# Attention and MLP on one core: batch 0 with products of zeros on TensorE, its masks and first bias rows made by TensorE, and loads issued head by head

## Chip, cores, metric

One Trainium2 chip, one NeuronCore. Times are device microseconds of a whole execution. The profiler's span of the same execution is shorter (390.0 beside 391.85). On one core, runs have no slow and fast die to compare; all runs here are of the state "fast", and yet those of one kernel spread by up to 6 us (before: 390.3 to 396.2).

## The reference, cut to what matters

```
# q, k, v: (8, 8, 576, 64), s: (8, 8, 576)
scores = q @ k.T / sqrt(D)
cum  = cumsum(max(s, 0)); bias = -(cum[i] - cum[j])        # "rows" c below
scores = where(causal, -1e9, scores + min(bias, 0))
attn = softmax(scores) @ v
x  = attn, heads side by side                               # (8, 576, 512)
xn = (x - mean) / sqrt(var + 1e-6) * g_ln
out = x + max(xn @ w_ch1, 0) @ w_ch2                        # 512 -> 2048 -> 512
```

## The kernel before

A head n (0 to 63) is: `scores` (products sa, sb, sc and sd of the four key blocks, exponentials by ScalarE), then, two heads later, `pv` (the weighted sum, into one PSUM buffer `pot`). From head 10 on, four MLP units of the batch before are woven into each head, so batch 0 (heads 0 to 7) and heads 8 and 9 stand alone. `qk_pair` transposes q and k of the next two heads. The bias enters as extra rows of q and k: cumulative sums split into c_hi, c_mid, c_lo.

```
def aug(gam, eng, last=None):            # bias rows of four heads: 4 DMAs, here from GpSimd
    eng.dma_start(out=kq[i][D+1:D+2, 0, :, 0:S], in_=c_hi[r0:r0+G, :])   # ... three more
def qk_pair(g, k_eng, q_eng):
    tr = ps_t.tile([P, S], BF16, name="trqk", tag="tr")      # ps_t: 2 buffers, also sd and trx
    ...                                                      # 6 transposes, 2 copies by eng
def scores_d(b, j):
    ...                                                      # 2 products, 1 exponential
    nc.gpsimd.affine_select(out=ed, in_=ed, ...)             # mask on GpSimd
...
aug(0, nc.gpsimd, nc.scalar)                                 # c_lo's row from ScalarE's queue
for n in range(BH):
    pre(n)                                                   # loads, casts, fills of that head
    if n < 10:
        scores(b, h)
        if h % 2 == 0: scores_d(b, h // 2)
        if n % 2 == 0 and n < 8:
            g = n // 2 + 1
            qk_pair(g, "dve", "dve" if g % 2 else "act")
        if n == 9:
            for t in range(NF): ln_tr(0, t)                  # transposes of xn
            queue += batch_units(0)                          # MLP units of batch 0
        if n > 1: pv_next()
        if n == 8: pv_next(); qk_pair(5, "act", "act")
        continue
    ...                                                      # cut: heads 10 to 63
```

The softmax here doesn't subtract the row's maximum and nothing guards it: scores larger than these inputs give would overflow.

## Time and profile before

| | before |
|---|---|
| median of the first runs | 393.6 us |
| span of the profile | 390.0 us |
| first score (sa of head 0) | 13.07 us |
| scores of head 8 | 39.65 us |
| first product of the MLP | 50.97 us |
| TensorE busy, share of the span | 92% |

Read the last line with care: busy is not fast. The clock column gives TensorE's granted clock, but here it reads 1.00 until its first recorded change at 39.53 us; before that the speed has to be read from distances between starts (from sa to its mask 0.40 us for head 5, 0.22 for head 8), as the prediction does. The lines are in the prediction.

### The profile page before, as it was taken

What the parts mean: (1) busy time and instruction counts of PE and PEld (TensorE: products, weight loads), DVE (VectorE), ACT (ScalarE), POOL (GpSimd) and SP (SyncE); (2) the same over time, 40 slices, a digit from 0 to 9 for tenths busy, and PEclk for the clock granted to TensorE, in tenths of its full rate; (3) what the DMA queues carried; (4) which work ended last, traced back from release to release, by engine and by line L of the source; (5) the groups of instructions that cost most, each with busy time, mean ns of one, the idle gap of its engine ahead of it and who ended that gap; (6) DMA issues with size and microseconds to landing.
All of it is one profiled execution on the core that took longest, in us unless ns stands there. A gap on an engine that the chain in (4) does not pass through costs nothing.

```text
span 390.0 us, 8129 instructions
## 1 busy us (share of the span) xinstructions
PE 360.7 (92%) x2959; PEld 199.4 (51%) x2959; DVE 202.5 (52%) x530; ACT 189.7 (49%) x359; POOL 177.6 (46%) x473
## 2 busy tenths in 40 slices
PE   1598699897999999999999999999999979999994
PEld 0376555454555555555555555655555534444441
DVE  7347745859643745484437545843665483212211
ACT  3476758574685356436743774277337400411400
POOL 5897359465656264636466656454742110000000
PEclk9999879999999999999999999999999989999998
DMA  8999799256886898749896998599820011002013
GB/s 190 223 155 206 132 129 152 30 105 155 184 180 125 143 242 184 173 118 234 180 166 158 236 177 195 141 213 170 195 92 4 2 54 55 2 28 81 2 34 73
DMA packets 148335, 51.84 MB, mean 133 GB/s; under 512 B 134696, under 2 KB 143496, under 8 KB 148296
## 3 DMA queue, kind: packets, MB, share of 16 engines
q1 hardware_dynamic: 139168, 44.07, 51.9%
q0 software_dynamic: 9120, 7.25, 12.5%
q8 instruction: 23, 0.38, 0.4%
q14 instruction: 16, 0.13, 0.1%
q10 hardware_dynamic: 8, 0.00, 0.0%
HBM read 37.11 MB, written 9.44 MB: 119 GB/s over the span
## 4 chain that ended last, share of the span: by engine, by line
PE 79%; DVE 10%; DMA 5%; ACT 2%; SPq 1%; issue 1%; POOL 0%; ACTq 0%; DVEq 0%
PE py L448 30%; PE ph L430 27%; PE pot L343 7%; PE sa L274 3%; PE sb L274 3%; PE sc L274 3%; DVE xn L401 2%; DVE kq L96 2%; PE trx L417 2%; DMA vtmp<-in_v_dram 2%; PE trqk L227 1%; SPq L149 1%; DMA kq<-c_lo 1%; DMA kq<-rows 1%; ACT er L285 1%
## 5 line engine op out<-in xcount | busy, mean ns | idle before, releaser
L448 PE MATMUL py<-w_bf,hT 128*128 128x512 bf16 x576 | 137.9, 381 | 2.5 <-DVE yo L457 2.2
L430 PE MATMUL ph<-xT,w_bf 128*128 128x512 bf16 x512 | 122.7, 381 | 1.2 <-DVE hT L438 1.0
L440 ACT ACTIVATE hT<-ph 128x512 bf16<-128x512 f32 x107 | 64.0, 598 | 83.4 <-PE ph L430 82.7
L430 PEld LDWEIGHTS <-w_bf 128*128 128x128 bf16 x576 | 52.1, 98 | 55.2 <-issue 5.6
L448 PEld LDWEIGHTS <-hT 128*128 128x128 bf16 x576 | 52.1, 98 | 52.5 <-issue 3.6
L285 ACT ACTIVATE er<-sa 128x512 bf16<-128x512 f32 x64 | 38.1, 596 | 79.2 <-PE sa L274 48.1
L293 POOL TENSOR_SCALAR_AFFINE_SELECT er<-er 128x128 bf16<-128x128 bf16 x216 | 59.5, 300 | 31.2 <-ACT er L285 31.0
L438 DVE TENSOR_SCALAR hT<-ph 128x512 bf16<-128x512 f32 x37 | 25.6, 691 | 58.0 <-PE ph L430 55.2
L161 POOL CAST rows<-rowtmp 128x512 bf16<-128x512 f32 (+1 forms) x50 | 30.5, 610 | 48.9 <-DMA rowtmp<-in_q_dram 46.2
L274 PEld LDWEIGHTS <-kq 68*128 68x128 bf16 x440 | 34.7, 102 | 34.6 <-POOL v_bf L98 5.5
L343 PEld LDWEIGHTS <-er 128*128 128x128 bf16 x960 | 40.0, 102 | 15.2 <-DVE xm L360 2.1
L351 DVE RECIPROCAL rinv<-pot 128x5 f32<-128x5 f32 x64 | 12.4, 194 | 61.1 <-PE pot L343 60.9
L343 PE MATMUL pot<-v_bf,er 128*128 128x65 bf16 x960 | 42.4, 199 | 1.7 <-DVE xm L360 1.7
L285 ACT ACTIVATE er<-sc 128x512 bf16<-128x512 f32 x64 | 38.9, 608 | 0.3
L285 ACT ACTIVATE er<-sb 128x512 bf16<-128x512 f32 x64 | 38.2, 596 | 0.0
L457 DVE SCALAR_TENSOR_TENSOR yo<-py,rstd,xb 128x512 f32<-128x512 f32 x32 | 23.8, 748 | 25.5 <-PE py L448 20.3
L98 POOL CAST v_bf<-vtmp 128x512 bf16<-128x512 f32 (+1 forms) x40 | 24.3, 616 | 17.4 <-DMA vtmp<-in_v_dram 17.3
L274 PE MATMUL sa<-kq 68*128 68x512 bf16 x64 | 26.5, 414 | 6.1 <-DMA kq<-c_lo 5.4
L353 DVE TENSOR_TENSOR xb<-pot,rinv 128x256 f32<-128x256 f32 x64 | 27.2, 425 | 2.2
L274 PE MATMUL sc<-kq 68*128 68x256 bf16 (+1 forms) x208 | 27.9, 244 | 0.1
L96 DVE COPY kq<-trqk 64x576 bf16<-64x576 bf16 x24 | 19.2, 800 | 14.9 <-PE trqk L227 14.5
L274 PE MATMUL sb<-kq 68*128 68x64 bf16 (+1 forms) x168 | 26.7, 261 | 0.2
(81 smaller groups left out, 301.9 us busy)
## 6 DMA issues: line engine op xcount, KB each, us to landing
vtmp<-in_v_dram SPq DMA_DIRECT2D x32, 256.0 KB, 4.2
out_dram<-yo SPq DMA_DIRECT2D x32, 256.0 KB, 2.2
rowtmp<-in_k_dram SPq DMA_DIRECT2D x40, 128.0 KB, 3.0
rowtmp<-in_q_dram SPq DMA_DIRECT2D x40, 128.0 KB, 3.2
w_bf<-in_moe_w_ch_dram POOLq DMA_DIRECT2D x8, 512.0 KB, 9.2
kp<-in_k_dram POOLq DMA_DIRECT2D x10, 144.0 KB, 4.1
qp<-in_q_dram POOLq DMA_DIRECT2D x10, 144.0 KB, 4.8
vtmp<-in_v_dram SPq DMA_DIRECT2D x8, 128.0 KB, 3.2
```

The source lines that it names most:

```text
L96: nc.vector.tensor_copy(out=out, in_=in_)
L98: nc.gpsimd.tensor_copy(out=out, in_=in_)
L161: nc.gpsimd.tensor_copy(out=r[0:pn, :, :, 0:D], in_=loaded.pop(("rows", gam, t))[0:pn])
L274: nc.tensor.matmul(a[:, c + a0 - q0 : c + a1 - q0], lhsT=k_cols(b, h, kb), rhs=cols, start=True, stop=not (pe_mask and diag),)
L285: nc.scalar.activation(out=e[:, o : o + 512], in_=a, func=ACT.Exp, scale=scale)
L293: nc.gpsimd.affine_select(out=e[:, o : o + P], in_=e[:, o : o + P], compare_op=ALU.is_ge, fill=0.0, base=0, pattern=[[1, P]], channel_mult ...
L343: nc.tensor.matmul(pot[:, t, :], lhsT=e[:, o : o + P], rhs=vv[:, kb, h, :], start=(kb == 0), stop=(kb == last),)
L353: nc.vector.tensor_tensor(out=xb[b][:, :, hs], in0=pot[:, 0:NF, 0:D], in1=rinv[:, 0:NF].unsqueeze(2).to_broadcast([P, NF, D]), op=ALU.mult,)
L430: nc.tensor.matmul(ph, lhsT=w1_bf[:, kd, fb * P : (fb + 1) * P], rhs=xT[:, kd, :], start=(kd == 0), stop=(kd == KD - 1),)
L438: nc.vector.tensor_scalar_max(out=hT[:, fb, :], in0=ph, scalar1=0.0)
L440: nc.scalar.activation(out=hT[:, fb, :], in_=ph, func=ACT.Relu)
L448: nc.tensor.matmul(py[0], lhsT=hT[:, fb, t * P : (t + 1) * P], rhs=w2_bf[:, fb, :], start=(fb == 0), stop=(fb == FB - 1),)
```

## The change

Intent: let TensorE's clock be granted early, by products of zeros while it would wait; make head 0's bias rows by small products instead of a DMA; take the masks of sd off GpSimd; and issue the loads in smaller portions. The diff, cut to its core:

```
+    def keep_warm(n):
+        w = ps_t.tile([P, 512], F32, name="idle", tag="tr")
+        for _ in range(n):
+            nc.tensor.matmul(w, lhsT=zeros[:, 0:P], rhs=zeros, start=True, stop=True)
@@ start
+    keep_warm(9)
-    aug(0, nc.gpsimd, nc.scalar)
+    aug(0, nc.sync, h0=1)                                   # heads 1 to 3 only
     qk_pair(0, "dve", "act")
+    # head 0: rows by 8 products with `pick`, keep_warm(4) among them, 4 copies out of PSUM
+    keep_warm(5)
@@ qk_pair:  batch 0 and pairs 4, 5 in the MLP's PSUM banks
+            if g < 6: tr = ps_m.tile([P, S], BF16, name="trqk", tag="m")
@@ scores_d: masks of batch 0 by a product with maskT, no affine_select
@@ pre(n):   aug on SyncE; one load per head (w1 at 0, 2, 4, 6; v of batch 1 at 6; w2 at 7 to 10)
+        elif n == 1:
+            nc.vector.memset(kq[1][D:KA, 1].bitcast(F32), ONE2)   # was GpSimd's, at n == 0
+            aug(1, nc.sync)
@@ loop
-                qk_pair(g, "dve", "dve" if g % 2 else "act")
+                qk_pair(g, "dve", "act")
+            if n < 8: keep_warm(2)
-            if n > 1: pv_next()
+            if n > 1 and n != 9: pv_next()                  # head 8's pv moves behind two units
             if n == 8: pv_next()
+                keep_warm(5)
```

More of the change, by code (lines that the diff above doesn't have):

```diff
@@ L87 @@
     xTm = const.tile([P, KD, 512], BF16, name="xTm")
-    c_hi = const.tile([BH, S], BF16, name="c_hi")
-    c_mid = const.tile([BH, S], BF16, name="c_mid")
-    c_lo = const.tile([BH, S], BF16, name="c_lo")
+    c3 = const.tile([BH, 3, S], BF16, name="c3")
+    c_hi, c_mid, c_lo = (c3[:, j, :] for j in range(3))
+    zeros = const.tile([P, 512], BF16, name="zeros")
+    ones = const.tile([BH, S], BF16, name="ones")
+    pick = const.tile([BH, 4, P], BF16, name="pick")
     def copy_on(eng, out, in_):
@@ L188, in ld_w2, with aug @@
         )
-    def aug(gam, eng, last=None):
-        r0 = gam * G
+    def aug(gam, eng, h0=0):
+        r = slice(gam * G + h0, gam * G + G)
         i = gam % 2
-        eng.dma_start(out=kq[i][D + 1 : D + 2, 0, :, 0:S], in_=c_hi[r0 : r0 + G, :])
-        eng.dma_start(out=kq[i][D : D + 1, 1, :, 0:S], in_=c_hi[r0 : r0 + G, :])
-        eng.dma_start(out=kq[i][D + 2 : D + 3, 0, :, 0:S], in_=c_mid[r0 : r0 + G, :])
-        (last or eng).dma_start(
-            out=kq[i][D + 3 : D + 4, 0, :, 0:S], in_=c_lo[r0 : r0 + G, :]
-        )
+        eng.dma_start(out=kq[i][D : D + 1, 1, h0:G, 0:S], in_=c_hi[r, :])
+        for j in range(3):
+            eng.dma_start(out=kq[i][D + 1 + j : D + 2 + j, 0, h0:G, 0:S], in_=c3[r, j, :])
     def bias_rows():
@@ L223, in qk_pair @@
             src = ready.pop((kind, g))
-            tr = ps_t.tile([P, S], BF16, name="trqk", tag="tr")
+            if g < 6:
+                tr = ps_m.tile([P, S], BF16, name="trqk", tag="m")
+            else:
+                tr = ps_t.tile([P, S], BF16, name="trqk", tag="tr")
             for t in range(QT):
@@ L304, in scores_d @@
         u0 = (2 * j) % 4
+        pe_mask = b * H + 2 * j < NM
         ed = er[0:TL, u0 : u0 + 2, OD : OD + TL]
@@ L312, in scores_d @@
                 start=True,
-                stop=True,
+                stop=not pe_mask,
             )
+            if pe_mask:
+                nc.tensor.matmul(
+                    d[:, u, :], lhsT=ident, rhs=maskT[:, 0:TL], start=False, stop=True
+                )
         nc.scalar.activation(out=ed, in_=d[0:TL], func=ACT.Exp, scale=scale)
+        if pe_mask:
+            return
         nc.gpsimd.affine_select(
@@ L504 @@
         ld_pair("q", g)
-    ld_v(0, 0)
-    ld_v(0, 1)
+    for t in range(3):
+        ld_v(0, t)
     ONE2 = 1.0019378662109375
     NEG2 = -1.0058441162109375
+    nc.vector.memset(zeros.bitcast(F32), 0.0)
     nc.vector.memset(warm, 0.0)
     nc.scalar.activation(out=warm[:, 1:2], in_=warm[:, 0:1], func=ACT.Exp)
+    keep_warm(9)
     nc.vector.memset(c_one, 1.0)
+    nc.vector.memset(pick.rearrange("p j m -> p (j m)").bitcast(F32), 0.0)
+    for j in range(3):
+        nc.vector.memset(pick[0:1, j, j + 1 : j + 2], 1.0)
+    nc.vector.memset(pick[0:1, 0, 32:33], 1.0)
+    nc.vector.memset(pick[0:1, 3, 0:1], -1.0)
+    nc.vector.memset(ones.bitcast(F32), ONE2)
     nc.vector.memset(kq[0][0:KA, 0, :, S:SP], 0.0)
-    nc.vector.memset(kq[0][D:KA, 1].bitcast(F32), ONE2)
+    nc.scalar.copy(
+        out=kq[0][D:KA, 1, :, 0:S], in_=ones[0:4].unsqueeze(1).to_broadcast([4, G, S])
+    )
     make_identity(nc, ident)
@@ L526 @@
     nc.gpsimd.memset(kq[0][D : D + 1, 0].bitcast(F32), NEG2)
+    ld_cast_pair(2)
     def v_edges(i):
@@ L544 @@
     nc.vector.tensor_tensor(out=c_lo, in0=c_in, in1=c_mid, op=ALU.subtract)
-    aug(0, nc.gpsimd, nc.scalar)
+    aug(0, nc.sync, h0=1)
+    ld_v(0, 3)
     qk_pair(0, "dve", "act")
-    ld_v(0, 2)
-    ld_v(0, 3)
+    ba = ps_s.tile([P, 512], F32, name="ba", tag="s")
+    bb = ps_s.tile([P, 512], F32, name="bb", tag="s")
+    for j, src in ((3, ones), (0, c_hi), (1, c_mid), (2, c_lo)):
+        if j == 2:
+            keep_warm(4)
+        nc.tensor.matmul(
+            ba, lhsT=pick[:, j, :], rhs=src[:, 0:512], start=(j == 3), stop=(j == 2)
+        )
+    for j, src in ((3, ones), (0, c_hi), (1, c_mid), (2, c_lo)):
+        nc.tensor.matmul(
+            bb[:, 0:TL], lhsT=pick[:, j, :], rhs=src[:, 512:S], start=(j == 3), stop=(j == 2)
+        )
+    nc.vector.tensor_copy(out=kq[0][D:KA, 0, 0, 0:512], in_=ba[0:4])
+    nc.scalar.copy(out=kq[0][D : D + 1, 1, 0, 0:512], in_=ba[32:33])
+    nc.vector.tensor_copy(out=kq[0][D:KA, 0, 0, 512:S], in_=bb[0:4, 0:TL])
+    nc.scalar.copy(out=kq[0][D : D + 1, 1, 0, 512:S], in_=bb[32:33, 0:TL])
+    keep_warm(5)
     cast_pair("k", 1, "pool")
@@ L551 @@
     ld_v(0, 4)
-    ld_cast_pair(2)
+    ld_cast_pair(3)
     v_edges(0)
@@ L555 @@
         cast_v(0, t, "pool")
-    nc.sync.dma_start(out=gb, in_=moe_g_ln.partition_broadcast(P))
     nc.gpsimd.memset(er[TL:P, :, OD : OD + TL], 0.0)
@@ L562, in pre @@
         if n == 0:
-            ld_cast_pair(3)
-            nc.gpsimd.memset(kq[1][D : D + 1, 0].bitcast(F32), NEG2)
-            nc.gpsimd.memset(kq[1][D:KA, 1].bitcast(F32), ONE2)
-            nc.gpsimd.memset(kq[1][0:KA, 0, :, S:SP], 0.0)
             nc.vector.memset(mhalf, -0.5)
+            nc.vector.memset(kq[1][0:KA, 0, :, S:SP], 0.0)
+            nc.vector.memset(kq[1][D : D + 1, 0].bitcast(F32), NEG2)
+            ld_w1(0)
         elif n == 1:
-            aug(1, nc.gpsimd)
+            nc.vector.memset(kq[1][D:KA, 1].bitcast(F32), ONE2)
+            aug(1, nc.sync)
             ld_cast_pair(4)
         elif n == 2:
-            ld_w1(0)
+            nc.sync.dma_start(out=gb, in_=moe_g_ln.partition_broadcast(P))
+            ld_w1(1)
+        elif n == 3:
             v_edges(1)
-            ld_v(1, 0), ld_v(1, 1), ld_v(1, 2), ld_v(1, 3), ld_v(1, 4)
-        elif n == 3:
-            ld_cast_pair(5)
-        elif n == 4:
+        elif n == 4:
+            ld_w1(2)
+        elif n == 5:
+            ld_cast_pair(5)
+        elif n == 6:
+            ld_w1(3)
+            ld_v(1, 0), ld_v(1, 1), ld_v(1, 2), ld_v(1, 3), ld_v(1, 4)
+        elif n == 7:
+            ld_w2(0)
+        elif n == 8:
+            ld_cast_pair(6)
+            ld_w2(1)
             cast_v(1, 0, "pool")
             cast_v(1, 1, "pool")
-        elif n == 5:
-            ld_w1(1)
+        elif n == 9:
+            ld_w2(2)
             cast_v(1, 2, "pool")
@@ L584, in pre @@
             cast_v(1, 4, "pool")
-        elif n == 6:
-            ld_cast_pair(6)
-        elif n == 7:
-            ld_w1(2)
-            ld_w1(3)
-        elif n == 9:
-            ld_cast_pair(7)
-            ld_w2(0)
-        elif n == 10:
-            ld_w2(1)
-            ld_w2(2)
-        elif n == 11:
+        elif n == 10:
+            ld_cast_pair(7)
             ld_w2(3)
@@ L609, in pre @@
         if n % 4 == 0 and 2 <= n // 4 + 1 < 2 * NPE:
-            aug(n // 4 + 1, nc.gpsimd)
+            aug(n // 4 + 1, nc.sync)
         for gam in range(2 * NPE, NG):
@@ L656 @@
                 g = n // 2 + 1
-                qk_pair(g, "dve", "dve" if g % 2 else "act")
+                qk_pair(g, "dve", "act")
+            if n < 8:
+                keep_warm(2)
             if n == 9:
@@ L661 @@
                 queue += batch_units(0)
-            if n > 1:
+            if n > 1 and n != 9:
                 pv_next()
@@ L675 @@
         run_units(1)
-        if n != 10:
-            pv_next()
+        pv_next()
         pend.append((b, h))
```

## The prediction

> **What bounds the kernel now.** I read the page's forty slices first, then the busy time by stretch, then the instructions in order of time up to 56 us, and last the chain that ended last.
>
> ```profile
> PE   1598699897999999999999999999999979999994
> PEclk9999879999999999999999999999999989999998
> DMA  8999799256886898749896998599820011002013
> ```
>
> One digit is 9.75 us. From the sixth slice on the PE row is nearly all nines: the MLP keeps TensorE full, and what lies there can't be shortened by this change. Room is in the first five slices, before the first product of the MLP (50.97 us). The stretches from 5.40 us, of 3.41 us each (start:end, length, PE busy, count, granted clock, DMA share, GB/s):
>
> ```profile
> 22.47:25.88 3.41, 3.40 (x37) 1.00 0.91 121
> 25.88:29.29 3.41, 3.10 (x32) 1.00 0.92 129
> ...
> 36.12:39.53 3.41, 3.41 (x42) 1.00 1.27 214
> 39.53:42.95 3.42, 2.49 (x53) 1.00 1.25 213
> 42.95:46.36 3.41, 1.79 (x25) 1.00 0.80 132
> 46.36:49.77 3.41, 2.30 (x28) 0.50 0.01 2
> 49.77:53.19 3.42, 3.42 (x15) 0.50 0.80 94
> ```
>
> Busy PE is not fast PE. The clock column says 1.00 up to 46 us, yet the timeline shows the products at half speed until 39.5 us (start us, duration):
>
> ```profile
> 29.68 0.62 PE L274 MATMUL sa<-kq 68*128 68x512 bf16 x1
> 30.08 0.31 PE L282 MATMUL sa<-maskT,ident 128*128 128x128 bf16 x1
> ...
> 39.65 0.38 PE L274 MATMUL sa<-kq 68*128 68x512 bf16 x1
> 39.87 0.22 PE L282 MATMUL sa<-maskT,ident 128*128 128x128 bf16 x1
> ```
>
> From sa to its mask takes 0.40 us for head 5 and 0.22 us for head 8: the clock column has no entry before its first change, and TensorE ran cold from the start to 39.5 us, again from 46.36 to 53.19. So batch 0 (heads 0 to 7, 13.07 to 39.65 us, 26.6 us, 6.65 a pair of heads) is bound by a cold TensorE, and the first score waits for something else:
>
> ```profile
> 13.07 0.59 PE L274 MATMUL sa<-kq 68*128 68x512 bf16 x1 [5.36 <-DMA kq<-c_lo]
> ...
> 44.94 2.66 DVE L401 SCALAR_TENSOR_TENSOR xn<-xb,mv,gb 128x512 bf16<-128x512 f32 x4
> 48.68 0.85 DVE L422 COPY xT<-trx 128x512 bf16<-128x512 bf16 x2 [0.34 <-PE trx L417]
> ```
>
> The bias rows come by DMA, 4.7 us after their issue at 8.15. Between head 8 and the MLP the bound is VectorE: weighted sums of heads 6 and 7, statistics, xn, xT, 40.75 to 49.5 us.
>
> [...] the changes at 39.53, 46.36 and 53.19 lie two windows of 3.413 us apart, release followed windows that were wholly busy (3.41, 3.42), one with 3.10 did not release, and 1.79 busy of 3.41 throttled while 1.94 (from 90.74) did not. [...] Up to 44 us the DMA share here is 0.9 to 1.3[...].
>
> **The change part by part.** All cold and warm costs are distances between starts in the timeline.
>
> *Start.* Nine products of zeros (9 x 0.427 = 3.8 us cold, from about 1.2 us when their zeros are written) end before the first transposes (5.9), and hold a whole window only for one phase in eight (3.84 - 3.41 of 3.41). Head 0's rows no longer come by DMA but by products: q's transposes end at 7.6 as now; then three products of 512 (1.28), four of zeros (1.71), the c_lo product (0.43), four of 64 columns (0.2), five of zeros (2.1): 13.3 us if cold, hardly better than 13.07. These 5.7 us are unbroken, so a free-running window fills somewhere between 10.5 and 13.9; after that the rest takes half. First score between 12.0 and 13.3, mean 12.6: gain 0.5 us. The copies out of PSUM (VectorE free at 9.7, c_lo product, 0.6 and 0.3) end by 12.0 and don't bind. The 2304-wide copy of ones on ScalarE (about 2.2 us, estimated from 0.60 for 512 and 0.83 for 768) ends near 5.1, about when k's load allows the cast anyway (5.02).
>
> *Heads 0 to 7, warm.* Per pair, TensorE: scores with masks 2 x 0.9, sd with its new masks 0.2, twelve transposes 0.52, two weighted sums 2 x 0.46, four products of zeros 4 x 0.215: 4.3 us. ScalarE: six exponentials at the 0.485 spacing of head 8 (40.19, 40.68, 41.16), sd 0.27, q's copies 1.61: 4.8. VectorE: k's copies 1.6, two heads of 0.98, statistics 0.9 to 1.4: 4.4 to 5.0. So the bound passes from TensorE (6.65) to ScalarE and VectorE at about 4.9, for all four pairs, as all q copies are now on ScalarE. Following the queues by hand from 12.8, with one weighted-sum buffer, scores(8) can start at 32.3 instead of 39.65. The masks of sd leave GpSimd (0.3 us each), which was no bound.
>
> *Taken back in there.* The bias rows of heads 4 to 7 wait on VectorE for a fill that now stands behind k's copies (about 17 us by my count), are then issued four times 0.52 us and land 3.4 to 6.9 us after (range in the trace): 22.5 to 25. Head 4 would want them at 22.0. I put down 1.2 us for that, and 0.3 for waits I can't see: scores(8) at 33.7.
>
> *Head 8 to the MLP.* The VectorE chain stays: 10.78 us from the exponentials of head 8 (40.19) to the MLP (50.97). Weighted sums of head 8 move behind the first two units: cold they took 0.84 us on the path, later they cost 0.46 warm. Five products of zeros fill only 1.1 us of a stretch where about 3.9 us of TensorE time hold 1.0 us of work; I expect the clock to be throttled there again in most phases, and 1.5 to 2.5 us lost on it, as now ((53.19 - 48.06) / 2 = 2.5). First MLP product about 10.3 us after scores(8): 44.0.
>
> *After.* TensorE is full from there, as many products as before plus the weighted sum moved: 50.97 - 44.0 - 0.46 = 6.5 us, rounded to 6.6 for a slightly shorter cold stretch: 393.6 - 6.6 = 387.0. The loads "one head at a time": only program order paces GpSimd's issues, and with the sd masks gone nothing holds it; four loads of weights enter the queue between about 16 and 22 us instead of 23.9 to 37.7.
>
> **Rivals.**
> (1) *DMA takes over.* Up to 45 us the engines are busy at a share near 1.2, with the same bytes needed 7 us earlier, and the last pair of q and k (issued behind three weight loads) is wanted near 36.6 us; my count has it landing between 31 and 36.5. For: GB/s falls to 121 only in one stretch, so there is little slack. Against: the weights of the later blocks (w2) aren't needed until 66 us, and v of batch 1 not until 45. If it binds, 2 to 5 us of the gain are lost: 389 to 391.
> (2) *The products of zeros cost more than they give.* If the window does not fill before head 0, cold pairs cost 6.4 + 4 x 0.43 = 8.1 us[...].
> (3) *The clock stays up throughout.* If the five products carry it over the xn stretch, some 2 us more are won, and with the bias rows in time another 1.2: 383 to 384. For it speaks that 1.94 us of work in a window sufficed.
> (4) *The gain is given back later.* In the region of 250 to 272 us the chain runs through row loads (vtmp, rows); but SyncE's queue there waits for outputs made by TensorE, so it moves with the start, and TensorE was busy 110 of 110 us from 140 to 250. I count little for it.
>
> **Range and chances.** The middle, 387.0, is the sum. Everything good (3) gives 383, DMA or bias rows late give 391. Two per cent is 385.8, within 1.2 us of my number: faster 0.35, same 0.63, slower 0.02, as only a fault that I don't see could cost over 14 us net.
>
> **What would show it.** Right: from sa to its mask 0.22 us from head 0 or 1 on; first score at 12 to 13.3; scores(8) at 32.5 to 35; exponentials of heads 2 to 7 back to back on ScalarE except ahead of head 4, where TensorE waits for the kq rows; first MLP product at 43 to 45; a granted clock of 0.50 at some time between 40 and 48; the MLP part unchanged in length. Wrong: a cold head 0 to 3, waits of trqk on kp or qp (rival 1), a first MLP product outside 42 to 46, or a gain at the end that differs from the gain at the first MLP product by over 1.5 us.

50.97 - 44.0 - 0.46 is 6.5 us, put at 6.6, and 393.6 - 6.6 = 387.0. Rival (2) came to 389. That another issuer of the bias rows shortens no transfer was not shown. The windows are the stretches of 3.413 us between which the clock changes in the traces (last section). That a filled one releases it was read from two of them (3.41 and 3.42 us of work), so what the *Start* says of it (one phase in eight, filled between 10.5 and 13.9, a first score as early as 12.0) is the author's estimate from these.

## The result

Median 387.44 us (387.33 to 387.59, 4 runs) beside 393.26 (391.32 to 393.66, 4 runs): ratio 0.9862, interval 0.9828 to 0.9896. A ratio here is the mean of one kernel's runs over the mean of the other's of the same rounds, so not quite the ratio of the medians. A second set of six runs gave 0.9869 (0.9823 to 0.9915; medians 387.56 and 392.61). By the 2% rule: the same; by the interval: faster by 1.0 to 1.7%.

The page after, the lines that answer to those of before:

```profile
PE   7878798997999999999999999999999979999994
PEclk9889899999999999999999999999999989999999
DMA  8799996178795599759887996589620011002013
```

The first, second and fifth slices of PE are fuller, the clock now has 8s in slices 2, 3 and 5 (the dips are in the record, as the first change comes early), and the rest is as before. From sa of head 0 to its mask:

```profile
12.14 0.38 PE L276 MATMUL sa<-kq 68*128 68x512 bf16 x1
12.36 0.22 PE L284 MATMUL sa<-maskT,ident 128*128 128x128 bf16 x1
...
24.46 0.38 PE L276 MATMUL sa<-kq 68*128 68x512 bf16 x1 [2.40 <-DMA kq<-c]
...
28.17 0.62 PE L276 MATMUL sa<-kq 68*128 68x512 bf16 x1
28.57 0.31 PE L284 MATMUL sa<-maskT,ident 128*128 128x128 bf16 x1
```

0.22 us: head 0 is warm. Head 4 (24.46) waits 2.40 us for its bias rows, and head 5 (28.17 to 28.57, 0.40) is cold again. The stretches of 3.41 us, laid so that their ends fall on the changes of the clock, show why (columns as in the prediction):

```profile
1.51:4.93 3.42, 3.42 (x9) 1.00 0.78 212
4.93:8.34 3.41, 2.06 (x18) 1.00 1.11 258
8.34:11.75 3.41, 3.41 (x13) 0.50 1.27 237
...
21.99:25.41 3.42, 1.02 (x14) 1.00 1.19 178
25.41:28.82 3.41, 3.41 (x39) 0.50 1.14 189
28.82:32.23 3.41, 3.41 (x53) 1.00 1.22 194
...
42.47:45.89 3.42, 1.74 (x18) 1.00 1.22 198
45.89:49.30 3.41, 3.41 (x21) 0.50 1.24 232
```

(Up to the first recorded change, here at 4.93 us, the column reads 1.00 while the products run at half speed, 0.43 us each, where four of 512 columns take 0.86 at full speed; the first of these stretches is the nine products of zeros.) A stretch with 1.02 or 1.74 us of work is followed by one at half clock; here a full one ends it. Busy time in the trace does not sort the stretches, though: one with 2.06 us (4.93 to 8.34) was also followed by half clock, one with 1.94 in the kernel before (from 90.74) was not, and there a stretch with 3.40 of 3.41 us of work (22.47 to 25.88) did not release the clock. More of them are at the end of this document; what sorts them is not shown.

Where the time went, in stretches between starts of sa, from each kernel's one profile. The last five columns are experiments that follow. Between heads 20 and 63 all are within 0.4 us of each other, so the whole matter is decided outside it. These are single profiles: those of f and c are of their slowest runs (388.76 us, 3.4 above the median of f, and 387.38), that of a is of its second slowest (388.82), that of j of its fastest.

| us | before | after | a no zeros | c rows early | f w2 late | j best | k gaps only |
|---|---|---|---|---|---|---|---|
| start to head 0 | 13.07 | 12.14 | 11.37 | 13.24 | 13.37 | 12.15 | 11.51 |
| head 0 to 8 | 26.58 | 23.40 | 24.80 | 19.64 | 19.38 | 19.73 | 22.65 |
| 8 to 11 | 16.44 | 16.67 | 17.53 | 17.60 | 17.35 | 14.50 | 14.37 |
| 11 to 14 | 15.16 | 15.15 | 15.16 | 15.15 | 15.15 | 13.96 | 13.97 |
| 14 to 18 | 16.52 | 16.52 | 16.52 | 18.19 | 16.52 | 16.53 | 16.52 |
| 18 to 20 | 12.07 | 12.08 | 12.07 | 12.08 | 15.13 | 12.10 | 12.08 |
| 20 to 63 | 204.07 | 203.82 | 203.84 | 203.83 | 204.19 | 203.79 | 203.82 |
| 63 to end | 86.09 | 85.92 | 85.81 | 85.87 | 85.91 | 84.24 | 84.18 |
| span | 390.0 | 385.7 | 387.1 | 385.6 | 387.0 | 377.0 | 379.1 |

Before to after: 0.93 us at the start and 3.18 in heads 0 to 8, and nothing between heads 8 and 14. By the profiles 4.3 us are won, and 5.8 by the medians.

### The profile page after: what moved, and what is told of

It reads as the page before. It is cut to its first block, busy times and chain, and to the rows that moved or that the text cites. A ratio compares the mean times of both kernels' runs of the same rounds, so it can differ in the third digit from the quotient of the medians.

```text
span 385.7 us, 8249 instructions
## 1 busy us (share of the span) xinstructions
PE 363.9 (94%) x3016; PEld 197.3 (51%) x3016; DVE 202.5 (53%) x538; ACT 194.5 (50%) x366; POOL 161.6 (42%) x442
## 4 chain that ended last, share of the span: by engine, by line
PE 80%; DMA 8%; DVE 5%; ACT 3%; SPq 1%; issue 1%; POOL 0%; ACTq 0%; DVEq 0%; POOLq 0%
PE py L457 31%; PE ph L439 30%; DMA vtmp<-in_v_dram 7%; PE pot L352 6%; PE sc L276 3%; PE sb L276 3%; PE sa L276 3%; PE trx L426 2%; ACT er L287 2%; DVE xn L410 2%; ACT kq L96 1%; DMA pairtmp<-in_q_dram 1%; PE trqk L229 1%; DMA kq<-c 1%; DVE yo L466 1%
## 5 line engine op out<-in xcount | busy, mean ns | idle before, releaser
L295 POOL TENSOR_SCALAR_AFFINE_SELECT er<-er 128x128 bf16<-128x128 bf16 x216 | 58.4, 294 | 33.3 <-ACT er L287 33.3
L352 PEld LDWEIGHTS <-er 128*128 128x128 bf16 x960 | 38.3, 99 | 17.9 <-DVE xm L369 3.1
L276 PEld LDWEIGHTS <-kq 68*128 68x128 bf16 x440 | 32.8, 98 | 27.6 <-DMA kq<-c 2.5
L352 PE MATMUL pot<-v_bf,er 128*128 128x65 bf16 x960 | 40.6, 195 | 2.3 <-DVE xm L369 1.8
L96 ACT COPY kq<-trqk 64x576 bf16<-64x576 bf16 x28 | 22.5, 802 | 11.9 <-PE trqk L229 11.7
L276 PE MATMUL sa<-kq 68*128 68x512 bf16 x64 | 24.6, 385 | 3.0 <-DMA kq<-c 2.4
L276 PE MATMUL sc<-kq 68*128 68x256 bf16 (+1 forms) x208 | 25.2, 232 | 0.2
L386 DVE BATCH_NORM_STATS2 stats<-xb 128x6 f32<-128x128 f32 (+1 forms) x96 | 25.0, 320 | 0.4
```

The costliest lines, as they stand in the source:

```text
L96: nc.scalar.copy(out=out, in_=in_)
L276: nc.tensor.matmul(a[:, c + a0 - q0 : c + a1 - q0], lhsT=k_cols(b, h, kb), rhs=cols, start=True, stop=not (pe_mask and diag),)
L295: nc.gpsimd.affine_select(out=e[:, o : o + P], in_=e[:, o : o + P], compare_op=ALU.is_ge, fill=0.0, base=0, pattern=[[1, P]], channel_mult ...
L352: nc.tensor.matmul(pot[:, t, :], lhsT=e[:, o : o + P], rhs=vv[:, kb, h, :], start=(kb == 0), stop=(kb == last),)
```

## The experiments

"Before" is run in the same rounds each time; its runs spread from 390.3 to 396.2 us. Kernels of the same rounds share those runs (a to d; e, f, g and i; h, j, k and the second "after").

**a: no products of zeros.**

```
     def keep_warm(n):
+        return
```

> The changed kernel with every product of zeros taken out, all else kept. Theory (the clock is the gain): TensorE is cold through most of batch 0 again, sa to its mask 0.40 us for heads 0 to 5, a pair of heads near 6.5 us; first score about 1 us earlier (11.2) as nothing stands in its way, scores of head 8 near 38 instead of 35.54, first MLP product near 48 instead of 45.5; time 390 (389 to 391.5). Rival (the gain is from the bias rows and the moved loads, the zeros are idle work): 387.5 or less.

Measured: median 387.79 (385.79 to 388.88), ratio 0.9859 (0.9802 to 0.9915): the gain of the whole change, without its zeros. The theory's number fails, and the rival's (387.5 or less) is missed too, by 0.3 us at the median. In its profile head 0 starts 0.8 us earlier than with zeros, batch 0 is cold at first, as expected, but only until 22.7:

```profile
22.31 0.57 PE L276 MATMUL sa<-kq 68*128 68x512 bf16 x1
22.72 0.22 PE L284 MATMUL sa<-maskT,ident 128*128 128x128 bf16 x1
22.78 0.38 PE L276 MATMUL sb<-kq 68*128 68x64 bf16 x2
23.00 0.22 PE L284 MATMUL sb<-maskT,ident 128*128 128x128 bf16 x1
```

From sa to its mask is still 0.41, from sb to its mask 0.22: the clock came in between, 17 us sooner than before (22.7 beside 39.5), from real work alone. (The clock fell again from 36.36 to 50.01: this profile is 3.5 us ahead of before at head 8, but only 2.4 at head 11.) So the zeros are one way to the clock, and the rest of the change another.

**b: no zeros in heads 0 to 7, the others kept.**

```
-            if n < 8:
-                keep_warm(2)
```

> The changed kernel without the two products of zeros per head in heads 0 to 7; those before head 0 and after head 7 stay. Theory: once released the clock stays, because real work fills about 3.4 of 4.9 us of a pair (0.70, above the 0.57 that kept it elsewhere), so nothing is lost: 387.4 within 0.6. Rival: without them the clock falls within heads 1 to 3 and a pair costs 6.5 us until it recovers: 389 or more.

Measured: 390.63 (390.27 to 392.25), ratio 0.9946 (0.9888 to 1.0004). The theory (no loss) fails; the rival's number holds, though not by its story: in its profile the clock did not fall in heads 1 to 3. It fell at 25.0, in the same wait of head 4 (2.37 us, until 26.63), and stayed down for two stretches:

```profile
21.58:25.00 3.42, 1.70 (x30) 0.99 1.23 184
25.00:28.41 3.41, 1.78 (x11) 0.50 1.13 175
28.41:31.82 3.41, 3.41 (x40) 0.51 1.21 201
...
35.24:38.65 3.41, 1.71 (x32) 0.99 1.22 197
38.65:42.06 3.41, 2.48 (x37) 0.50 1.23 195
42.06:45.48 3.42, 3.42 (x22) 0.51 1.24 195
```

In the profile of the changed kernel each dip lasted one stretch, as the next one was full. Head 0 also started at 14.81, as in that run the clock was down from 7.87 to 14.69. How the 3.2 us share out over these I can't say from one profile.

**d: the zeros alone, in the kernel before.** The transposes go to other PSUM banks; no run has the zeros without that.

```
+            if g < 6: tr = ps_m.tile([P, S], BF16, name="trqk", tag="m")
+    keep_warm(9) at the start, keep_warm(9) after qk_pair(0),
+    keep_warm(2) in heads 0 to 7, keep_warm(5) after head 7's pv
```

> The kernel before with the products of zeros alone (nine at the start, nine after the first transposes, two per head, five after head 7) and with the transposes of q and k in the MLP's PSUM banks, which the zeros need. Theory (the clock is the gain): first score unchanged at 13.1, heads 0 to 7 at 5 to 5.5 us a pair, scores of head 8 near 35, time 389.5 (388 to 391). Rival (the zeros only pay with the rest of the change): 392 or more.

Measured: 387.88 (387.18 to 391.68), ratio 0.9886 (0.9821 to 0.9952). The theory holds by its ratio (389 from 393.4, in its range) but not by its steps: its profile, which fell on the slowest of the four runs, has the scores of head 8 at 38.21, not near 35, and heads 0 to 8 in 25.69 us instead of 26.58. So by the ratios zeros with banks give most of the gain, everything but zeros gives all of it, and both together give no more. That the two replace each other is the simplest reading. The intervals of a, d and the whole change overlap, so differences under 2 us between them are not shown.

**i: banks and ScalarE copies alone, no zeros.**

```
+            if g < 6: tr = ps_m.tile([P, S], BF16, name="trqk", tag="m")
-                qk_pair(g, "dve", "dve" if g % 2 else "act")
+                qk_pair(g, "dve", "act")
```

> The kernel before with two small parts of the change alone: the transposes of q and k of batch 0 go to the MLP's PSUM banks, and q's copies are all on ScalarE (before, every second pair's were on VectorE, 3.3 us for the four copies). No products of zeros. Theory, formed after the run without zeros kept the gain: TensorE no longer waits for VectorE's copies, so its own cold work fills a whole window at heads 2 to 3 and the clock is released near 22 to 26 us instead of 39.5; scores of head 8 at 36.5 to 38, time 389.5 (388 to 391). Rival: the release without zeros came from the masks of sd, the bias rows or the loads, so this kernel stays at 392 or more.

Measured: 391.38 (388.32 to 391.89), ratio 0.9938 (0.9872 to 1.0003): at most a part. The theory falls: the clock came at 33 us, not at 22 to 26, for TensorE had waits that run a did not have or had shorter (start, duration, idle before):

```profile
22.23 0.29 PE L346 MATMUL pot<-v_bf,er 128*128 128x65 bf16 x2 [0.70 <-POOL er L319]
24.49 1.00 PE L346 MATMUL pot<-v_bf,er 128*128 128x65 bf16 x15 [0.26 <-DVE xm L363]
28.18 0.58 PE L277 MATMUL sa<-kq 68*128 68x512 bf16 x1 [2.68 <-DMA kq<-c_lo]
```

Head 4's rows, issued by GpSimd behind its other work, came at 28.2; in a at 25.7. What of the rest of a (rows by products, loads, masks) makes its full stretch at heads 2 and 3 is not separated further.

**e: head 0's rows by DMA again.**

```
-    aug(0, nc.sync, h0=1)   and the 8 products and 4 copies of ba, bb
+    aug(0, nc.sync)
```

> The changed kernel with head 0's bias rows by DMA again (all four heads in the four transfers on SyncE; the eight products and four copies out of PSUM go, the nine products of zeros there stay). Theory: the rows land when those of heads 1 to 3 land now (sd waited for them until 13.92), so the first score is at 13.9 instead of 12.14, but head 4 waits for its own rows anyway (until 24.46), so little of the 1.8 us is seen at the end: 388.0 (387.2 to 389). Rival: the start is on the path in full, 389.2 or more.

Measured: 388.41 (387.09 to 389.41), ratio 0.9886 (0.9837 to 0.9935), as expected in time. Head 0 at 14.19 instead of 12.14, head 8 at 35.78 instead of 35.54: of 2.05 us, 0.24 are left in this profile, of the fastest run. The reason is not the one expected. Head 4 still waits, but its rows come later too:

```profile
26.01 0.38 PE L276 MATMUL sa<-kq 68*128 68x512 bf16 x1 [2.06 <-DMA kq<-c]
```

So 1.55 us are still missing at head 4 (26.01 instead of 24.46). The rest comes back behind it: heads 4 to 8 take 9.77 us instead of 11.08, for here the clock does not fall after the wait (its dip is at 14.98 to 18.39). Here the wait (23.95 to 26.01) lies across the end of a window at 25.22; in the changed kernel (22.06 to 24.46) it lies within one (21.99 to 25.41). That this is the cause is the author's reading, and how the windows lie cannot be counted on.

**h: the masks of sd on GpSimd again.**

```
-        pe_mask = b * H + 2 * j < NM
+        pe_mask = False            # in scores_d
```

> The changed kernel with the masks of the last key block (sd) of batch 0 on GpSimd again. Theory: those five masks are off the path (0.3 us each on an engine that is idle there), and their waits pace GpSimd's weight loads again, so v of batch 1 may come a little earlier: within 0.8 us of the changed kernel of the same rounds. Rival: a weighted sum waits for GpSimd's mask (0.7 us once in the kernel before with two parts), over 1 us slower.

Measured: 387.43 (386.59 to 387.84), ratio 0.9866, beside 0.9869 for the changed kernel of the same rounds. As expected; this part is worth nothing that shows.

**c: rows of heads 4 to 7 early.**

```
     nc.vector.memset(kq[0][0:KA, 0, :, S:SP], 0.0)
+    nc.vector.memset(kq[1][D:KA, 1].bitcast(F32), ONE2)     # was in pre(1)
@@ pre(0)
+            aug(1, nc.sync)                                  # was in pre(1)
```

> The changed kernel with the fill of the ones rows of heads 4 to 7 moved into VectorE's idle 1.1 us before c_in lands, and their bias rows issued by SyncE before head 0 instead of at head 1. Theory: the 2.40 us wait of head 4 for the kq rows goes, and with it the cold stretch of 25.4 to 28.9 us (about 1 us lost): scores of head 8 near 32.3, time 384.3 (383.3 to 385.3). Rival: the DMA engines are the limit behind it, v of batch 1 (cast at 48.6 to 49.9) or a pair of q, k then binds, and no more than 1 us is won: 386.4 or more.

Measured: 387.14 (385.48 to 387.38), ratio 0.9839 (0.9791 to 0.9887): the rival's number. But the profile shows both at work. The wait of head 4 and its dip are gone, heads 0 to 8 take 19.64 us (theory), and 3.0 us are won at head 10. Then 1.36 us go to the weighted sum of head 8, which waits for v of batch 1 (rival):

```profile
46.89 0.28 PE L352 MATMUL pot<-v_bf,er 128*128 128x65 bf16 x4 [0.62 <-POOL v_bf L100]
47.67 0.31 PE L352 MATMUL pot<-v_bf,er 128*128 128x65 bf16 x5 [0.50 <-POOL v_bf L100]
48.22 0.19 PE L352 MATMUL pot<-v_bf,er 128*128 128x65 bf16 x1 [0.24 <-POOL v_bf L100]
```

and 1.67 at head 14 to a dip of the clock (65.75 to 69.16 us) that the profile of the changed kernel does not have: both have a wait of 1.0 us at head 13, where VectorE fills cT, and the stretch with the wait has 2.38 us of work in both (62.34 to 65.75 in c, 62.95 to 66.36 in the changed kernel). Why the clock fell only in c is not shown.

**f: c, and the second weights behind v.**

```
-            ld_w2(0) at head 7, ld_w2(1) at 8, ld_w2(2) at 9
+            for i in range(3): ld_w2(i)                      # in pre(10)
```

> The early rows of heads 4 to 7 (c_rows_early) and the first three loads of the second weight matrix moved behind the casts of v of batch 1. Theory: in c_rows_early 1.36 us of the 3.0 us won at head 10 were lost to the weighted sum of head 8 waiting for v casts, because weights that are needed 20 us later fill the DMA queue; with them out of the way v lands before 44, head 11 starts near 49.1 instead of 50.48, time 385.8 (384.5 to 386.8). Rival: v is late because SyncE's queue issues it late, and head 11 stays at 50.3 or later.

Measured: 385.38 (383.98 to 388.76), ratio 0.9823 (0.9758 to 0.9889). The waits for v are gone from its list; head 11 at 50.10 instead of the 49.1 expected, as in this run the dip between heads 8 and 11 lasted two stretches (40.92 to 47.74). The theory holds for v, but of the 1.4 us expected at head 11 only 0.38 came. The profile is that of the slowest run. In the same profile another dip, of two stretches, costs 3.05 us at heads 18 to 20.

**g: f, and zeros in the gap of xn; VectorE's cT fills at head 10.**

```
                 for t in range(NF):
+                    if t == 2: keep_warm(8, ps_m, "m")
                     ln_tr(0, t)
```

> f_w2_late, and eight products of zeros between the second and third transpose group of xn (in the MLP's PSUM bank), and VectorE's two fills of cT moved from head 13 to head 10. Theory: the clock stays granted from head 8 to head 11 (now a dip of 3.4 us, about 1.6 us lost), and the 1.0 us wait of the MLP for hT at head 13, which lets the clock fall in some runs, goes: head 11 near 47.8, time 383.3 (382 to 384.5). Rival: the dip costs little, as TensorE waits for VectorE there anyway: within 1 us of f_w2_late.

Measured: 385.24 (384.33 to 386.51), ratio 0.981 (0.976 to 0.9859). By time within 1 us of f, which is the rival's number; by the profile not its reason. From head 8 to 11 it takes 14.50 instead of 17.35 us, and head 11 is at 46.54, better than expected. But a dip at heads 18 to 20 (87.46 to 90.87) cost 1.72 us that c's profile did not lose, and I had put the three loads of w2 ahead of a pair of q and k, which came back as waits:

```profile
56.39 0.43 PE L229 MATMUL trqk<-ident,kp 96*128 96x96 bf16 x6 [1.12 <-DMA kp<-in_k_dram]
57.48 0.43 PE L229 MATMUL trqk<-ident,qp 96*128 96x96 bf16 x6 [0.67 <-DMA qp<-in_q_dram]
```

**j: g, the pair ahead of the weights, zeros in the two other gaps.**

```
-            for i in range(3): ld_w2(i)
             ld_cast_pair(7)
-            ld_w2(3)
+            for i in range(4): ld_w2(i)
@@ n == 19, before qk_pair, and after ln_tr(7, 0) at the end
+            keep_warm(9, ps_s, "s")
```

> g_gap_zeros with the last early pair of q and k loaded ahead of the second weight matrix (its 1.8 us wait at head 13 was made by me), and products of zeros also in the two other gaps of TensorE: nine at head 19 (a wait of 2.1 us for xT) and nine in the last layer norm (2.25 us for yo). Theory: what the clock costs is dips that fall on full TensorE work; with every gap over 1.5 us filled there are none from head 3 on, so the time is the dip-free sum: head 11 near 46.5, head 14 near 60.7, time 379.7 (378.5 to 381.5), spread of the runs under 1 us. Rival: gaps are slack only in appearance, zeros push the real work or only move the dips: 383 or more.

Measured: 379.55 (378.67 to 380.37, 6 runs), ratio 0.9673 (0.9625 to 0.972), and beside the changed kernel in the same rounds 379.57 / 387.46 = 0.980 by the means. The time is as the theory had it (heads 11 and 14 at 46.37 and 60.34 too); the spread of 1.7 us is smaller than that of the changed kernel (2.3) but not the "under 1 us" expected. TensorE's waits in the whole profile (total, times, longest), first of the changed kernel:

```profile
PE sa L276 <- DMA kq<-c: 2.4, 1, 2.4
PE py L457 <- DVE yo L466: 2.2, 1, 2.2
PE trqk L229 <- DVE xT L431: 2.1, 1, 2.1
PE pot L352 <- DVE xm L369: 1.8, 2, 0.9
PE trx L426 <- DVE xT L431: 1.7, 1, 1.7
...
PE ph L439 <- DVE hT L447: 1.0, 1, 1.0
```

then of j:

```profile
PE pot L352 <- DVE xm L369: 2.5, 4, 0.9
...
PE sd L311 <- DMA kq<-c: 0.7, 1, 0.7
PE sa L276 <- ACT er L287: 0.6, 1, 0.6
PE trx L426 <- DVE xn L410: 0.5, 2, 0.3
PE py L457 <- DVE yo L466: 0.3, 1, 0.3
```

The waits for yo and xT are not shorter in truth; zeros stand in their place (heads 18 to 20 take 12.10 us beside 12.08). What they give is the clock: in this profile no dip is recorded from 11.5 us to the last product of the MLP.

**k: j with the zeros in the gaps only.**

```
-    keep_warm(9) at the start, keep_warm(4) and keep_warm(5) at head 0, keep_warm(2) in heads 0 to 7
```

> j_best without the zeros at the start, between the bias products and in heads 0 to 7; only those in the gaps after head 7 stay. Theory: TensorE's own cold work releases the clock by head 3 (22.5 us in the run without zeros), first score near 11.5, head 8 near 33.5 instead of 32; 381.2 (379.7 to 382.7). Rival: without them the clock falls within heads 3 to 7 and head 8 is at 36: 384 or more.

Measured: 380.80 (380.46 to 381.25), ratio 0.970 (0.9647 to 0.9753), as expected; its clock came at 22.3 us and then stayed. So once the gaps after head 7 are filled, the zeros that the change added at the start and in its heads are worth 1.3 us (380.83 - 379.57 by the means).

**after, again.** The changed kernel, unedited, in the rounds of h, j and k.

> The changed kernel once more, beside the three below on one chip, to have it in other phases of the clock's window: 387.5 within 1.2, ratio 0.985 (0.982 to 0.988); the spread of its runs up to 2 us, as one dip of the clock more or less on full TensorE work is worth 1.6 us.

Measured: 387.56 (386.02 to 388.36, 6 runs), ratio 0.9869, as expected, with a spread of 2.3 us. In its profile head 0 is at 11.38 and no dip is recorded before 26.6, yet the dip at head 9 takes two stretches (43.66 to 50.49): the same program, another lie of the window (a change at 26.60 instead of 25.41).

## Why the prediction came out

The time was right: 387.0 forecast, 387.4 measured. Most of the mechanism was right too, but that the number fits so well is luck, as the sum below shows. By its steps:

- *Start*: 12.0 to 13.3 forecast, 12.14 measured, 11.38 in the second profile. In other runs with the same front zeros it was 12.13 (h) to 14.81 (b), with 13.24 and 13.37 in c and f; the lie of the window is the likely cause. "One phase in eight" for the nine first zeros was too low: in eight of nine profiles with zeros at the start (all but f; that of d is not counted) the clock was released before 6.2 us, also in c and g, where only 3.04 and 3.16 of 3.41 us were filled. The step took a wholly filled window for the condition. The prediction's own list shows that this was not it: next to the stretch with 3.10 it has one with 3.40 of 3.41 us that did not release, which the text passes over.
- *Heads 0 to 7 warm, the bound at ScalarE and VectorE at about 4.9 us a pair*: right in size, and for ScalarE. Heads 0 to 2 took 4.85 us, and with the wait of head 4 removed (j) the four pairs took 4.85, 4.91, 4.70 and 5.27. In the changed kernel ScalarE is busy 9.13 of the 9.92 us from head 0 to the wait of head 4 (12.14 to 22.06), VectorE only 5.90, and 13.55 of the 23.40 us of heads 0 to 8, so VectorE's 4.4 to 5.0 us a pair were put too high.
- *Taken back*: the wait of head 4 was named with its cause, and its landing (22.5 to 25) held at 24.4, as did the time at which head 4 would want it (22.0 forecast, 22.06), but 1.2 us was put down for it and it was 2.40. (32.3 + 1.2 + 0.3 is 33.8, not 33.7.) The step also missed that the clock would fall after so long a wait (25.41 to 28.82, after a stretch with 1.02 us of work). Together they put the scores of head 8 at 35.54 and not 33.7. This is the step of the prediction that was mis-sized most. Run c shows the size: without the wait, heads 0 to 8 take 3.8 us less.
- *Head 8 to the MLP*: 10.3 us forecast, 9.99 measured; a dip forecast between 40 and 48, measured 45.89 to 49.30. Before, it took 11.32 us from the scores of head 8; what is won here is mostly work moved, for from head 8 to 11 it takes 16.67 us beside 16.44. The first MLP product came at 45.53, outside the 43 to 45 that I gave, by what was lost at head 4.
- *After*: between heads 11 and 63 only 0.25 us are gained or lost, as forecast.
- *The sum*: 6.6 us forecast, 5.8 by the first medians. The spans differ by only 4.3, because the profile of before was of a run 1.4 us below its median. The working counted 6.6 us on that profile (391.85) and took them from a median (393.6). From the profiled run it would have given 385.2, and the profiled run of after took 387.35. So about 2 us lost at head 4 were offset by a median of before that is worse than the profile on which I counted. That is luck.

The reading that GB/s fell to 121 in one stretch only was too kind as well: the next one, in its own list, has 129. What the prediction did not see is that the zeros were not needed for the gain (run a). It took the slow clock of batch 0 for a state that only added work could end. But the same change also removed waits of TensorE, and then its real work filled a stretch by 22.7 us. By which of its parts is not shown. Of the rivals, DMA (1) was close behind, as written: it appears as 0.37 us in the changed kernel and as 1.36 in c, as soon as TensorE is 3 us earlier. Rival (3), 383 to 384 if the clock stays up, was not tested by itself; with every gap filled and the rows, weights and fills moved (j) it is 379.6.

Open: how much of a's early clock each of its parts gives. What makes a stretch release or lower the clock is not shown either; the stretches are listed below.

## What to carry to other kernels

Read TensorE's speed from distances between starts before you trust a busy share, and count dips of its clock as a cost of every wait: a wait of 2 us can cost 2 us plus half of each 3.4 us stretch at half clock that follows on full work (1.67 us for one such stretch in c, 3.05 for two in f). Fill waits where the work after them is dense, which is where zeros pay (here 6.3 us between f and j, 385.87 and 379.57 by the means, came with them, the earlier cT fills and the pair loaded ahead of the weights; f and j ran in different rounds), more than where another engine is the bound (1.3 us between k and j); and take out the waits themselves first, for real work releases the clock too (by 22.7 us in a). When a time spreads by some us from run to run, compare stretch by stretch in profiles, as one median can hide a gain in one stretch and a dip in another (c, g).

## TensorE's clock in these profiles

- *Where it changes.* In the kernel before, the recorded changes are at 39.53, 46.36, 53.19, 319.43, 322.84 and 387.70 us. They lie 6.83, 6.83, 266.24, 3.41 and 64.85 us apart: 2, 2, 78, 1 and 19 times 3.413. In the changed kernel (4.93 to 383.81 us) all distances are such multiples too. A "window" in this document is a stretch of that length laid on them.
- *From full to half clock.* Windows with 1.02, 1.74 and 2.06 us of work (after, 21.99 to 25.41, 42.47 to 45.89, 4.93 to 8.34) and with as much as 2.38 (c, 62.34 to 65.75) were followed by half clock, while one with 2.38 (after, 62.95 to 66.36), one with 1.94 (before, 90.74 to 94.15) and one with 1.57 (the second profile of after, 88.03 to 91.44) were not. So no threshold in busy time fits these.
- *From half to full clock.* Nine products of zeros alone (after, 1.51 to 4.93, 3.42 us) were followed by full clock, so zeros did release it. So were windows with 3.04 (c, 0.90 to 4.31), 3.16 (g, 2.12 to 5.54) and even 2.68 us (e, 8.15 to 11.56) of work, most of it zeros with 128 rows. Windows with 3.40 (before, 22.47 to 25.88) and with 3.41 (f, 6.79 to 10.20) were not: 1.5 us of the first are products of 68 rows, and the second has transposes and products of 64 rows among zeros. Whether the rows make the difference was not tested.
- *What it cost.* In the kernel before the first release came only at 39.53 us. Heads 0 to 8 took 26.58 us there and 19.73 in j, so the slow start cost up to 6.85 us, 1.8% of 390.0 (an estimate, as j has other changes too). Later dips cost 1.67 us (at head 14 in c) and 3.05 us (at heads 18 to 20 in f).
- *The clock column* had no value before the first recorded change: it read 1.00 in the kernel before while products ran at half speed until 39.5 us.
